# Scaling x before it is transposed, with prepared expert weights and a re-planned instruction order, in an attention, Sinkhorn-routing and expert kernel

## The chip, the cores and the metric

The kernel runs on one core of one Trainium2 chip. The metric is the device time of one execution, in microseconds (us); lower is better. Before the change, the first four runs gave a median of 1021.72 us (1018.52 to 1023.25).

## The reference

The program does attention with a window, then a mixture of eight experts in which every token passes through every expert, weighted by a Sinkhorn-normalised routing table.

```python
# q_l, k_l, v_l: 8 batches x 8 heads x 512 local tokens x 64;  q_g, k_g, v_g: 32 global tokens
# local queries see the global keys and a window of +-32; global queries see everything
x = attention(...)                      # 4352 tokens x 512
logits = x @ w_gate                     # 8 experts
P = np.exp(logits - logits.max())
for _ in range(8):                      # Sinkhorn: rows, then columns
    P /= P.sum(1, keepdims=True) + 1e-09
    P /= P.sum(0, keepdims=True) + 1e-09
    P *= N / E
out = np.zeros((N, D))
for e in range(E):
    h = np.maximum(x @ w1[e], 0.0)      # 512 -> 1024
    out += P[:, e:e + 1] * (h @ w2[e])  # 1024 -> 512
```

(The code is cut to what matters.) Since P is positive, `P * (relu(x @ w1) @ w2)` equals `relu((P * x) @ w1) @ w2`. The kernel uses this: it scales x, not the result.

## The kernel before

The program has four stages. **Attention** (32 pairs of heads) takes about the first 190 us. It is not limited by TensorE: each pair is a chain that passes between TensorE, ScalarE and VectorE. So the matmuls of **expert 0** are spread in its gaps; in the source and below they are called filler. Expert 0 is computed without its routing weight at that point (the weight is applied later), so it needs no routing. The **routing** follows: a serial chain of small VectorE steps and eight pairs of tiny TensorE column sums, `pcs`, again with expert 0 as filler. Then come 119 **units** (17 groups of 256 tokens, first with experts 1 to 3, then with 4 to 7), each made of 14 half-size products in the manner of Strassen. The **switch** between the two passes lies at about 540 to 640 us.

The order of instructions on every engine is fixed when the program is built, by a small list planner in the kernel. It works from planned durations and latencies, and each engine then runs its list in order:

```python
    def run_schedule(window=10**6):
        while pending:
            best = None
            for o in pending[:window]:
                ...
                t = ready(o)                       # when dependencies and buffers are planned free
                if t is None:
                    continue
                end, eng = min((max(t, free.get(e, 0.0)) + us, e) for e, us in o.eng.items())
                c = (max(t, free.get(eng, 0.0)), o.key)   # earliest start first, then priority
                if best is None or c < best[0]:
                    best = (c, o, eng, end)
            ...
            free[eng] = end
            o.end = end + o.lat
```

Attention operations have keys below 1000; expert 0's matmuls have keys from 1000 up, so they come second on a tie. The load of expert 0's weights (two transfers, 4 MB read) is planned as 12 us of the DMA queue:

```python
    def load_w0():
        nc.gpsimd.tensor_copy(out=tick, in_=stage[1, "q"][:, 0, 0:1])
        nc.gpsimd.dma_start(out=w1_0, in_=moe_w1[0].rearrange("(dko dki) f -> dki dko f", dki=P))
        nc.gpsimd.dma_start(out=w2_0, in_=moe_w2[0].rearrange("(fko fki) d -> fki fko d", fki=P))

    w0 = op("DMA", 12.0, load_w0, 3.6, [ops_load[1, "q", 0], ops_load[1, "k", 0]], lat=DMAL)
```

In the expert stage x is held transposed in DRAM (`xTd`), and VectorE multiplies it by the routing weights, which are broadcast over partitions (`pb`), twice per unit. The weights of experts 4 to 7 are loaded in halves of 512 KB by DMAs that convert from fp32 to fp16:

```python
    def prep(k, n_):
        ...
        if n_ < 2:
            pb = pbs[n, g][:, e - PASSES[n][0]].rearrange("p a c -> p (a c)")
            ks = slice(DK * n_, DK * (n_ + 1))
            nc.vector.tensor_tensor(out=x[:, ks], in0=xgs[n, g][:, ks],
                                    in1=pb.unsqueeze(1).broadcast_to([P, DK, 256]), op=ALU.mult)
        ...   # n_ 2 to 4: three sums and differences of x for the Strassen products

    def add_late_w(e, pool, tag, xpool, xtag, u0, before1, before2):
        at = TU * (u0 - 3)
        mk("LW1", e, "DMA2", 6.0, lambda: load_w1(e, pool(), tag), at, before1, lat=DMAL)
        mk("LW2", e, "DMA2", 6.0, lambda: load_w2(e, pool(), tag), at, [("LW1", e), *before2], lat=DMAL)
        ...   # then eight VectorE combinations of the weights
```

The softmax here doesn't subtract the row's maximum and nothing guards it: scores larger than these inputs give would overflow.

Of the kernel before, what the change touches and what calls it, by code (L numbers as in the profile page):

```python
# [17 lines left out]
def kernel(  # L18
# [51 lines left out]
    identity32 = persist.tile([P, P], FP32)  # L70
    xT = fill.tile([P, DP, NTOK], FP16, bufs=1)
# [6 lines left out]
    xTd = dram.tile([GN, P, DP, 256], FP16)  # L78
    ws = {}

    def load_w1(e, pool, tag=""):
        w1r = pool.tile([P, 4, DK, F // 2], FP16, tag="w1r" + tag, bufs=1, name="w1r")
        src = moe_w1[e].rearrange("(dko dki) f -> dki dko f", dki=P)
        for f in (0, 1):
            nc.gpsimd.dma_start(out=w1r[:, 2 * f : 2 * f + 2].rearrange("p a k x -> p (a k) x"),
                                in_=src[:, :, F // 2 * f : F // 2 * (f + 1)])
        ws[e] = [w1r, None, None]

    def load_w2(e, pool, tag=""):
        wb = ws[e][1] = pool.tile([P, 7, FK, Dhalf], FP16, tag="wb" + tag, bufs=1, name="wb")  # L90
        src = moe_w2[e].rearrange("(fko fki) d -> fki fko d", fki=P)
        for c in (0, 1):
            nc.gpsimd.dma_start(out=wb[:, 2 * c : 2 * c + 2].rearrange("p a k x -> p (a k) x"),
                                in_=src[:, :, Dhalf * c : Dhalf * (c + 1)])
# [28 lines left out]
    def op(eng, us, fn, key, deps=(), alloc=None, uses=(), lat=0.15):  # L123
        o = Op()
        o.eng = eng if isinstance(eng, dict) else {eng: us}
        o.fn, o.key, o.deps, o.alloc, o.lat, o.end = fn, key, [x for x in deps if x is not None], alloc, lat, None
        users[o] = [o]
        for u in uses:
            if u is not None:
                users[u].append(o)  # L130
                o.deps.append(u)
        pending.append(o)
        return o
# [3 lines left out]
    def ready(o):  # L137
        t = 0.0
        for x in o.deps:
            if x.end is None:  # L140
                return None
            t = max(t, x.end)
        if o.alloc:
            tag, n = o.alloc
            h = heads.setdefault(tag, [])
            if len(h) >= n:
                for x in users[h[-n]]:
                    if x.end is None:
                        return None
                    t = max(t, x.end)  # L150
        return t

    def run_schedule(window=10**6):
# [3 lines that stand above are left out]
# [6 lines left out]
                c = (max(t, free.get(eng, 0.0)), o.key)  # L163
                if best is None or c < best[0]:
                    best = (c, o, eng, end)
            (start, _), o, eng, end = best
# [7 lines left out]
    PEL, DMAL = 0.28, 2.2  # L174

# [20 lines left out]
    qkT, ugk, u_, xns, ogs, pts, pss, pgs, pos_, pqs, hTs, phs, pys = ({} for _ in range(13))  # L196
# [100 lines left out]
    def normalise(p):  # L297
# [3 lines left out]
        t = xns[p] = wk.tile([P, NM, 2, Dh], FP16, tag="xn", bufs=3, name="xn")  # L301
# [4 lines left out]
    xo = gbank[:, 0:256].bitcast(FP16)  # L306
    ptg = gbank[:, 384 : 384 + 2 * Sg].rearrange("p (a s) -> p a s", s=Sg)
# [15 lines left out]
    def normalise_g(b, hh):  # L323
        rg = wk.tile([P, 1], FP32, tag="rg", name="rg")
        nc.vector.reciprocal(out=rg, in_=pog[:, Dh:VC])
        t = ogs[b, hh] = wk.tile([P, Dh], FP16, tag="og", name="og")
        nc.vector.tensor_scalar(out=t, in0=pog[:, 0:Dh], scalar1=rg[:, 0:1], scalar2=None, op0=ALU.mult)

    def back(p):
        for m in range(NM):  # L330
            nc.tensor.transpose(xo[:, P * m : P * (m + 1)], xns[p][:, m, :, :], identity)
# [7 lines left out]
    def gate(t0, t1):  # L339
        for to in range(t0, t1):  # L340
            for dk in range(DP):
                nc.tensor.matmul(pl[:, (to - t0) * E : (to - t0 + 1) * E], xT[:, dk, P * to : P * (to + 1)],
                                 w_gate_sb[:, dk, :], start=(dk == 0), stop=(dk == DP - 1))

    def exp_gate(t0, t1):
        nc.scalar.activation(out=K_nat[:, t0:t1, :].rearrange("p t e -> p (t e)"),
                             in_=pl[:, 0 : (t1 - t0) * E], func=AF.Exp)
# [37 lines left out]
    GT = 4  # L385
    groups = [(t, min(GT, TO - t)) for t in range(0, TO, GT)]

    def h_unit(g, fm, half):
# [6 lines left out]
        for dk in range(2 * half, 2 * half + 2):  # L395
            nc.tensor.matmul(phs[g, fm][:, 0:TG], w1_0[:, dk, P * fm : P * (fm + 1)], xT[:, dk, P * g0 : P * g0 + TG],  # L396
# [19 lines left out]
    def evac_y(eng, g, c):  # L416
        t = yss[g, c] = (late["ys"] if "ys" in late else fill).tile([P, D], FP32, tag="ys", bufs=5 if "ys" in late else 2,
# [3 lines left out]
    def store_y(g, c):  # L421
        nc.gpsimd.dma_start(out=y0d[groups[g][0] + c], in_=yss[g, c])
# [3 lines left out]
    make_identity(nc, identity32)  # L426
# [22 lines left out]
    T, EQ, EK, SC, X, M, GK, XG, A, N, AG, NG, BK, EB, FL, EF, GA, GE, GO, XS = ({} for _ in range(20))  # L449
    LDORD = [(0, nm, n) for n in range(4) for nm in ("q", "k", "v") if nm != "v" or n % 2 == 1]  # L450

    def add_load(b, nm, n, of, key):
# [3 lines left out]
        ops_load[b, nm, n] = op("DMA", dma_us[nm] / of, lambda: load(b, nm, h0, h1), key, deps, lat=DMAL)  # L456
# [55 lines left out]
    def add_attend(p):  # L512
# [3 lines left out]
        A[p] = op("PE", 0.9, lambda: attend(p), k + 0.2, [M[p, 0], M[p, 1], ops_cast[b, "v", hp // 2], gv[b // 2]],  # L516
                  uses=[X[p, 0, 0], X[p, 0, 1], XG[b, hh]], alloc=("po", 1), lat=PEL)
        N[p] = op("DVE", 0.85, lambda: normalise(p), k + 0.2, uses=[A[p]], alloc=("xn", 3))
        BK[p] = op("PE", 0.24, lambda: back(p), k + 0.3, uses=[N[p]], alloc=("xo", 1), lat=PEL)
        EB[p] = op(either(0.49, 0.61), 0, lambda eng: copy_on(eng, xT[:, hp, S_tok * b + Sg : S_tok * (b + 1)], xo), k + 0.3,  # L520
                   uses=[BK[p]])
        if hp % 2 == 1:
            AG[b, hh] = op("PE", 0.36, lambda: attend_g(b, hh), k + 0.25, [A[p], XS[b // 2]],
                           uses=[X[p, 0, 0], X[p - 1, 0, 0]], alloc=("pog", 1), lat=PEL)
            NG[b, hh] = op("DVE", 0.4, lambda: normalise_g(b, hh), k + 0.25, uses=[AG[b, hh]], alloc=("og", 2))
            FL[b, hh] = op("PE", 0.15, lambda: flip(ptg, ogs[b, hh]), k + 0.35, uses=[NG[b, hh]], alloc=("ptg", 1), lat=PEL)
            EF[b, hh] = op("ACT", 0.15, lambda: nc.scalar.copy(
                out=xT[:, 2 * hh : 2 * hh + 2, S_tok * b : S_tok * b + Sg], in_=ptg), k + 0.35, uses=[FL[b, hh]])

    S_tok = Sg + Sl  # L530
# [7 lines left out]
    tick = const.tile([P, 1], FP32)  # L538

    def load_w0():  # L540
        nc.gpsimd.tensor_copy(out=tick, in_=stage[1, "q"][:, 0, 0:1])
        nc.gpsimd.dma_start(out=w1_0, in_=moe_w1[0].rearrange("(dko dki) f -> dki dko f", dki=P))
        nc.gpsimd.dma_start(out=w2_0, in_=moe_w2[0].rearrange("(fko fki) d -> fki fko d", fki=P))

    w0 = op("DMA", 12.0, load_w0, 3.6, [ops_load[1, "q", 0], ops_load[1, "k", 0]], lat=DMAL)
    add_load(1, "v", 0, 1, 3.7)

    ready_b, sched_gate = {}, 0
    for b in range(B):
# [17 lines left out]
        t0, t1 = sched_gate, (S_tok * (b + 1)) // P  # L567
        sched_gate = t1
        ready_b[b] = [EB[p] for p in range(HP * b, HP * (b + 1))] + [EF[b, 0], EF[b, 1]]
        GA[b] = op("PE", 0.55, lambda t0=t0, t1=t1: gate(t0, t1), HP * (b + 1) + 0.6, ready_b[b], alloc=("pl", 1), lat=PEL)  # L570
        GE[b] = op("ACT", 0.2, lambda t0=t0, t1=t1: exp_gate(t0, t1), HP * (b + 1) + 0.6, uses=[GA[b]])
# [11 lines left out]
    for n, (kind, g, i) in enumerate(seq):  # L583
        key = 1000.0 + n
        if kind == "h":
            us = 0.435 * groups[g][1] / GT
            if i == 0:
                htag = op("NONE", 0.0, lambda: None, -5, [w0], alloc=("hT", 2))
            u0 = op("PE", us, lambda g=g, i=i: h_unit(g, i, 0), key, [w0, *ready_b[min(g, B - 1)], before],
                    alloc=("mm", 2), uses=[htag])  # L590
            before = op("PE", us, lambda g=g, i=i: h_unit(g, i, 1), key, [u0], lat=PEL)
            r = op(either(0.5, 0.61), 0, lambda eng, g=g, i=i: relu_h(eng, g, i), -2, [before], uses=[u0])
            hops[g, i] = (u0, r, htag)
        else:
            prev = None
            for q in range(4):
                prev = op("PE", 0.435, lambda g=g, i=i, q=q: y_unit(g, i, q), key,
                          [before, *([hops[g, f][1] for f in range(FT)] if q == 0 else [prev])],
# [4 lines left out]
            ev = op(either(0.5, 0.61), 0, lambda eng, g=g, i=i: evac_y(eng, g, i), -2, [prev], uses=[first], alloc=("ys", 2))  # L603
# [3 lines left out]
    stored = []  # L607
    for g in range(GN):
        bs = range(256 * g // S_tok, (256 * g + 255) // S_tok + 1)
        stored.append(op("DMA", 0.7, lambda g=g: nc.sync.dma_start(out=xTd[g], in_=xT[:, :, 256 * g : 256 * (g + 1)]),  # L610
                         500.0 + g, [x for b in bs for x in ready_b[b]], lat=DMAL))
    all_att = [x for b in range(B) for x in ready_b[b]] + list(GE.values())

    def open_late():
# [3 lines left out]
        late["cp"] = late_pool("cp", bufs=2, side="right")  # L618
        late["ps_h"] = late_pool("ps_h", bufs=1, side="right", space=PSUM)
        late["sink"] = tc.alloc_tile_pool(name="sink", bufs=1, side="right", reuse_waits="tile")  # L620
        late["ps_c"] = tc.alloc_tile_pool(name="ps_c", bufs=1, space=PSUM, reuse_waits="tile")
        late["ys"] = tc.alloc_tile_pool(name="late_ys", bufs=1, reuse_waits="tile")
# [40 lines left out]
    R = TO * E  # L663
    ptd = dram.tile([TO, E, P], FP32)
    pn = P_nat.rearrange("p t e -> p (t e)")

    def turn(j):
        n = min(P, R - P * j)
        if j == 0:
            sk["pT"] = late["ps_c"].tile([P, 3, P], FP32, tag="cs", name="pT")  # L670
            sk["pT_sb"] = late["sink"].tile([P, 3, P], FP32, tag="pT", bufs=1, name="pT_sb")
        nc.tensor.transpose(sk["pT"][0:n, j, :], pn[:, P * j : P * j + n], identity32)

    def turn_out(j):
        n = min(P, R - P * j)
        nc.scalar.copy(out=sk["pT_sb"][0:n, j, :], in_=sk["pT"][0:n, j, :])
# [316 lines left out]
```

## Time and profile before

| | before |
|---|---|
| median of 4 runs | 1021.72 us |
| span of the profiled run | 1020.1 us |
| TensorE busy | 981.1 us (96%) |
| VectorE busy | 884.8 us (87%) |
| ScalarE busy | 672.1 us (66%) |
| moved by DMA | 119.18 MB |

These are the first line, the busy line and one line of the costliest groups from the page of the kernel before. A group's line reads: line, engine, operation, output and inputs, shape, count, then busy us in all and mean ns of one, then the engine's idle time before them and what ended it.

```profile
span 1020.1 us, 30644 instructions
...
PE 981.1 (96%) x12921; PEld 830.7 (81%) x12921; DVE 884.8 (87%) x2058; ACT 672.1 (66%) x1306; POOL 51.6 (5%) x89
...
L708 DVE TENSOR_TENSOR xp<-xg,pb 128x512 f16<-128x512 f16 x238 | 163.2, 687 | 15.4 <-PE Y L725 15.4
```

TensorE (PE) is busy nearly all the time, but its busy share hides differences between the stages. So the next view matters more: the windows view of the kernel before. Each row is a stretch of time, its length, the busy us of each engine with its number of instructions, the granted TensorE clock, the DMA share and GB/s.

```profile
core 0: us, PE busy (x) PEld busy (x) DVE busy (x) ACT busy (x) POOL busy (x), PEclk, DMA share, GB/s
...
30.00:70.00 40.00, 37.21 (x535) 21.55 (x533) 26.76 (x64) 29.16 (x64) 0.74 (x2) 0.87 0.89 247
70.00:190.00 120.00, 118.14 (x1850) 68.65 (x1849) 83.90 (x195) 91.60 (x206) 17.73 (x26) 1.00 0.76 194
190.00:300.00 110.00, 100.91 (x820) 64.24 (x819) 70.00 (x154) 57.50 (x109) 19.64 (x31) 0.97 0.70 156
300.00:540.00 240.00, 239.48 (x3219) 224.65 (x3217) 238.09 (x565) 168.22 (x320) 0.00 (x0) 1.00 0.29 92
540.00:640.00 100.00, 92.45 (x1203) 84.75 (x1200) 94.56 (x218) 60.63 (x116) 6.50 (x8) 0.98 0.55 122
640.00:1000.00 360.00, 360.00 (x4899) 341.62 (x4897) 342.65 (x803) 242.19 (x450) 0.00 (x0) 1.00 0.23 71
```

The reader should see three losses that look removable: VectorE at 238.09 of 240 us in the first pass, 92.45 of 100 us for TensorE at the switch, and 100.91 of 110 us around the routing. The next view shows what TensorE waited for at the switch (waits of TensorE, 540 to 640 us; us in total, times, longest):

```profile
PE X L725 <- ACT u3s L736: 3.0, 1, 3.0
PE X L725 <- DVE xp L708: 1.7, 2, 1.4
PE X L725 <- ACT u2s L736: 1.6, 3, 0.5
PE Z L725 <- DVE h L100: 0.9, 2, 0.5
```

A busy share does not tell a matmul at half clock from one at full clock. So I worked out a second number from the records. Each matmul is given the time that it needs at full clock: 0.417 ns for each of its columns plus 2 ns, an estimate fitted to the commonest spacing of starts in these traces (0.056 us for 128 columns, 0.109 for 256, 0.216 for 512); matmuls that use only part of the array's rows or columns are counted at their share. The **lost time** up to a moment is that moment minus the full-clock time of all the matmuls started by then. It adds up waits and half-clock time. It is an estimate, the same for all kernels, and between two profiles of one kernel it differs by up to 3 us.

| lost in, us | 0-190 (attention) | 190-300 (routing, first units) | 300-540 (pass 1) | 540-640 (switch) | 640-1000 (pass 2) |
|---|---|---|---|---|---|
| before | 67.6 | 16.0 | 5.0 | 12.4 | 2.3 |

### The profile page before, as it was taken

How to read it: one execution, taken by the hardware profiler on the slowest of the kernel's cores; microseconds unless marked ns; L12 is line 12 of the kernel's file. 1: busy time of each engine (PE TensorE's matmuls, PEld its weight loads, DVE VectorE, ACT ScalarE, POOL GpSimd, SP SyncE). 2: the span in 40 equal slices, each digit the busy share in tenths (PEclk: the TensorE clock that was granted, in tenths of full speed). 3: DMA queues.
4: the chain of work that ended last, by engine and by line, in shares of the span. 5: the costliest groups of instructions: out<-in, count | busy, mean ns of one | idle time of the engine just before them, and what ended most of it. 6: DMA issues, size and time to landing. Idle time of an engine off the chain costs nothing. (4 is left out here: it accounts for less than half of the span.)

```text
span 1020.1 us, 30644 instructions
## 1 busy us (share of the span) xinstructions
PE 981.1 (96%) x12921; PEld 830.7 (81%) x12921; DVE 884.8 (87%) x2058; ACT 672.1 (66%) x1306; POOL 51.6 (5%) x89
## 2 busy tenths in 40 slices
PE   5999999989999999999999889999999999999997
PEld 3555655434799999999999878999999999999997
DVE  5677776581599999999999899999999999999996
ACT  4678877434667766777776556666666666666664
POOL 2000030211300000000000100000000000000000
PEclk9799999989999999999999999999999999999999
DMA  9979696732962332332322791222222222222211
GB/s 266 259 219 296 203 209 135 132 119 96 226 143 80 99 94 85 94 94 93 104 76 91 141 195 59 90 73 74 74 74 74 75 74 74 74 75 73 75 43 43
DMA packets 127530, 119.18 MB, mean 117 GB/s; under 512 B 17424, under 2 KB 102944, under 8 KB 127392
## 3 DMA queue, kind: packets, MB, share of 16 engines
q1 hardware_dynamic: 99040, 91.13, 29.2%
q0 software_dynamic: 26768, 25.70, 13.4%
q8 instruction: 101, 1.65, 0.7%
q10 hardware_dynamic: 1584, 0.39, 0.2%
q14 instruction: 37, 0.30, 0.1%
HBM read 102.65 MB, written 31.33 MB: 131 GB/s over the span
## 5 line engine op out<-in xcount | busy, mean ns | idle before, releaser
L763 PE MATMUL acc<-wb,s 128*128 128x256 f16 x1904 | 275.4, 273 | 0.4 <-DVE s L100 0.3
L739 ACT ACTIVATE h<-h 128x512 f16<-128x512 f16 x357 | 224.3, 630 | 71.9 <-DVE h L100 70.1
L725 PEld LDWEIGHTS <-w1r 128*128 128x128 f16 x3808 | 245.3, 98 | 21.3 <-issue 12.4
L763 PE MATMUL acc<-wb,h 128*128 128x256 f16 x1428 | 209.9, 273 | 0.1
L725 PEld LDWEIGHTS <-w1x 128*128 128x128 f16 x2856 | 182.8, 98 | 5.3
L763 PEld LDWEIGHTS <-s 128*128 128x128 f16 x1904 | 172.5, 98 | 15.9 <-DVE s L100 0.6
L708 DVE TENSOR_TENSOR xp<-xg,pb 128x512 f16<-128x512 f16 x238 | 163.2, 687 | 15.4 <-PE Y L725 15.4
L725 PE MATMUL X<-tt,w1r 128*128 128x128 f16 x1904 | 145.5, 219 | 6.3 <-ACT u3s L736 4.6
L763 PEld LDWEIGHTS <-h 128*128 128x128 f16 x1428 | 130.2, 98 | 12.7 <-issue 1.0
L736 ACT COPY u3s<-X 128x512 f32<-128x512 f32 x119 | 69.3, 582 | 73.9 <-PE X L725 73.4
L100 DVE TENSOR_TENSOR h<-p1s,Z 128x512 f16<-128x512 f32 x119 | 81.2, 682 | 30.1 <-ACT p1s L736 28.1
L736 ACT COPY p1s<-X 128x512 f32<-128x512 f32 x119 | 69.1, 581 | 29.2 <-PE X L725 29.2
L100 DVE TENSOR_TENSOR h<-u3s,Y 128x512 f16<-128x512 f32 x119 | 81.3, 683 | 2.4 <-ACT u3s L736 2.1
L736 ACT COPY u2s<-X 128x512 f32<-128x512 f32 x119 | 68.5, 576 | 22.5 <-PE X L725 22.3
L100 DVE TENSOR_TENSOR h<-u2s,Y 128x512 f16<-128x512 f32 x119 | 81.1, 682 | 1.6 <-PE Y L725 1.6
L739 ACT ACTIVATE h<-X 128x512 f16<-128x512 f32 x119 | 70.1, 589 | 17.0 <-PE X L725 14.0
L252 ACT ACTIVATE u<-sc 128x480 f16<-128x480 f32 (+1 forms) x128 | 61.0, 523 | 22.5 <-PE sc L247 21.8
L396 PE MATMUL ph<-xT,w 128*128 128x512 f16 (+1 forms) x288 | 73.8, 373 | 1.8 <-ACT ys L200 1.1
L725 PE MATMUL X<-xp,w1r 128*128 128x128 f16 x952 | 72.6, 219 | 1.9 <-DVE xp L708 1.7
L725 PE MATMUL Z<-xp,w1r 128*128 128x128 f16 x952 | 72.6, 219 | 1.2 <-DVE h L100 1.0
L725 PE MATMUL Y<-tt,w1x 128*128 128x128 f16 x952 | 73.0, 220 | 0.0
L725 PE MATMUL X<-tt,w1x 128*128 128x128 f16 x952 | 72.6, 219 | 0.0
(121 smaller groups left out, 1299.0 us busy)
## 6 DMA issues: line engine op xcount, KB each, us to landing
pb<-ptd SPq DMA_DIRECT2D x119, 128.0 KB, 3.9
y0d<-ys POOLq DMA_DIRECT2D x34, 256.0 KB, 3.5
xg<-xTd SPq DMA_DIRECT2D x34, 256.0 KB, 3.6
o<-y0d SPq DMA_DIRECT2D x34, 256.0 KB, 2.8
ya<-o SPq DMA_DIRECT2D x34, 256.0 KB, 2.1
o<-ya SPq DMA_DIRECT2D x34, 256.0 KB, 3.1
out_dram<-o SPq DMA_DIRECT2D x34, 256.0 KB, 2.0
qs<-in_q_l_dram SPq DMA_DIRECT2D x7, 1024.0 KB, 7.8
```

Source lines behind the costliest of these rows:

```text
L100: nc.vector.tensor_tensor(out=o, in0=a, in1=b_, op=ALU.add)
L252: nc.scalar.activation(out=u_[p][i][:, mp, :], in_=pss[p, mp][i][:, 0:w], func=AF.Exp, scale=scale)
L396: nc.tensor.matmul(phs[g, fm][:, 0:TG], w1_0[:, dk, P * fm : P * (fm + 1)], xT[:, dk, P * g0 : P * g0 + TG], start=(dk == 0), stop=(dk == ...
L708: nc.vector.tensor_tensor(out=x[:, ks], in0=xgs[n, g][:, ks], in1=pb.unsqueeze(1).broadcast_to([P, DK, 256]), op=ALU.mult)
L725: nc.tensor.matmul(dst[:, j, :], l[:, d, P * j : P * (j + 1)], r[:, d, :], start=(first and j == 0 and d == 0), stop=(j == FK - 1 and d == ...
L736: nc.scalar.copy(out=d[k], in_=X[k])
L739: nc.scalar.activation(out=hq(k, f, t), in_=hq(k, f, t) if src is None else src, func=AF.Relu)
L763: nc.tensor.matmul(acc(i), l[:, j, :], wb[:, r, j, :], start=(e == es[0] and j == 0 and i in (1, 5)), stop=(e == es[-1] and j == FK - 1), ...
```

## The change

The intent is to take work off VectorE and to have the weights ready at the switch:

- x is stored to DRAM in natural layout, from attention's output. For each unit it is scaled there, one half on ScalarE and one half on VectorE, stored to a scratch tensor, and read back through a DMA transpose.
- The weights of experts 4 and 5 arrive in 128 KB pieces spread over pass 1. Those of 6 and 7 are converted to fp16 in DRAM in pass 1, and loaded at the switch by plain DMAs. The weights of experts 1 to 3 are converted by GpSimd.
- The planner is changed: the two w0 loads are planned on GpSimd with a long latency and take no DMA time; input loads are planned with a longer latency; dependencies between two TensorE operations lose their latency; and expert 0's matmuls carry a penalty (`PEN`), which holds them back during attention.

The core of the diff (848 lines; the rest is wiring, pool moves and the split of some groups of x between TensorE and DMA transposes):

```diff
-            t = max(t, x.end)
+            t = max(t, x.end - (x.lat if x.pe and o.pe else 0.0))
...
-                c = (max(t, free.get(eng, 0.0)), o.key)
+                c = (max(t, free.get(eng, 0.0)) + (PEN if o.pe and o.key >= 1000 else 0.0), o.key)
...
+    PEN = 0.2
...
-        ops_load[b, nm, n] = op("DMA", dma_us[nm] / of, lambda: load(b, nm, h0, h1), key, deps, lat=DMAL)
+        ops_load[b, nm, n] = op("DMA", dma_us[nm] / of, lambda: load(b, nm, h0, h1), key, deps, lat=2.2 if b == 0 else 5.0)
...
-    w0 = op("DMA", 12.0, load_w0, 3.6, [ops_load[1, "q", 0], ops_load[1, "k", 0]], lat=DMAL)
+    w0 = []
+    first = op("NONE", 0.0, lambda: None, -5, [ops_load[0, "v", 0]], lat=9.0)
+    for i in (0, 1):
+        w0 += 4 * [op("POOL", 0.9, lambda i=i: load_w0_gp(i), 3.6 + 0.01 * i, [first], lat=(13.0, 20.0)[i])]
...
+    def scale_x(eng, k, a):
+        ...
+        o, i, w = xss[k][:, a], xgs[n, g][:, a], P_nat[:, 2 * g + a, e : e + 1]
+        if eng == "ACT":
+            nc.scalar.activation(out=o, in_=i, func=AF.Copy, scale=w)
+        else:
+            nc.vector.tensor_scalar(out=o, in0=i, scalar1=w, scalar2=None, op0=ALU.mult)
+
+    def put_x(k):
+        nc.sync.dma_start(out=xsd[k % NX].rearrange("(a p) d -> p a d", p=P), in_=xss[k])
+
+    def turn_x(k):
+        xps[k] = late["cp"].tile([P, DP, 256], FP16, tag="xp", bufs=5, name="xp")
+        nc.sync.dma_start_transpose(out=xps[k], in_=xsd[k % NX])
...
-            nc.vector.tensor_tensor(out=x[:, ks], in0=xgs[n, g][:, ks], in1=pb.unsqueeze(1).broadcast_to([P, DK, 256]),
-                                    op=ALU.mult)
...
+    def cast_piece(e, i):            # experts 6 and 7: fp32 -> fp16 inside DRAM
+        d, src, n = (wd1, moe_w1, D // 8) if i < 8 else (wd2, moe_w2, F // 8)
+        r = slice(n * (i % 8), n * (i % 8 + 1))
+        nc.gpsimd.dma_start(out=d[e][r], in_=src[e][r])
```

## The prediction

> **What bounds the kernel now.** TensorE. The page gives it 981.1 us of 1020.1 busy (96%), VectorE 884.8 (87%), ScalarE 66%. By the matmul starts in the timeline, one work unit (256 tokens, one expert, fourteen products) takes 6.18 us from 640 to 1000 us, with a product starting every 0.44 to 0.45 us: this half is at its matmul rate, and the change keeps its 84 matmuls per unit. 119 units need 735.8 us; the expert stage takes 260 to about 1015.5 us, so 20 us are lost:
> - about 5 us in the first pass, where units from 12 to 30 take 6.34 us: the windows view shows VectorE busy 68.0 of 68.0 us (332 to 400);
> - about 11.5 us at the switch to experts 4-7 (560 to 640 us): waits of 2.99, 1.41 and several 0.5 us, on `u3s`, VectorE's `xp` multiply and `h`, while weights load (9.0 and 13.3 us per half); granted clock 0.93;
> - about 3 us at its start (waits of 1.28, 0.5, 0.34 us).
> Before it, 260 us hold attention, expert 0 and the routing. At 200 to 230 us TensorE waits 3.65 us behind a routing column sum (`pcs`), then gets clock 0.87. The first 50 us lose more (11.3 us idle in the first 25, clock 0.80 in the next 26), but mostly to input loads: DMA share 1.0.
>
> **What the change does.** Scaling by routing weights moves from transposed x (two VectorE multiplies per unit, 687 ns each, 163.2 us in all) to natural layout, on ScalarE or VectorE (planned 0.58 or 0.26 us per half); the result goes to DRAM and returns through a DMA transpose. Weights 4-7 are loaded in small throttled pieces beforehand, 6 and 7 converted in DRAM so that the switch needs only plain loads. Expert weights 1-3 are converted by GpSimd. Layer 1 of the first two units runs inside expert 0's tail. TensorE loses 16 of 128 transposes of `xn` and three of P (about 2 us in all).
>
> **On the critical path.** VectorE's load per first-pass unit falls by roughly 0.7 us or more, so that pass should go at 6.18: -5 us. The switch: two to four units of time for 512 KB plain loads, so -9. Sinkhorn/expert 0 and the transition: -6. Fewer TensorE transposes: -2. New stalls (GpSimd issuing in order, transpose latency, more HBM traffic, early stage): +1 to +4. The Trainium skill ("DMA: Bandwidth & Descriptors", Latency and other measured facts) gives a DMA transpose 261 GB/s; so I estimate 1 us of DMA time, plus about 4 to 5 us latency, per 6.18 us unit. No run here shows it yet. It is issued several units ahead, so it should stay hidden.
>
> **Prediction: 1000 us, range 986 to 1016.** Chances: faster by over 2% 0.57, within 2% 0.39, slower 0.04.
>
> **Right if** units of both passes take 6.18 us; VectorE falls below 85% in the first pass, total to some 750 us; no `xp` wait over 1 us; the switch loses under 3 us; no half-clock stretch at 566 us; the largest waits left lie in the first 60 us.
>
> **Wrong if** DMA transposes take over 6 us in throughput (units would stretch evenly, TensorE waiting for `xp` from DMA); in-order GpSimd delays `o` loads, so seeds of accumulators stall each group; attention slows under earlier DMA traffic or because `xT` for expert 0 comes late, leaving routing without matmuls to hide it.

## The result, and the profile after

| | before | after |
|---|---|---|
| median | 1021.29 us (16 runs, 1018.52 to 1025.16) | 1014.93 us (11 runs, 1013.23 to 1017.50) |
| ratio | | 0.9934, 95% interval 0.9921 to 0.9948 |
| profiled span | 1020.1 us | 1012.6 us |
| VectorE busy | 884.8 us (87%) | 803.1 us (79%) |
| ScalarE busy | 672.1 us (66%) | 735.9 us (73%) |
| moved by DMA | 119.18 MB | 179.30 MB |

A ratio is the mean time of one kernel's fast runs over that of the other's fast runs of the same rounds, so it is not quite the ratio of the medians quoted beside it. The change is worth 0.7%, not the forecast 2.1%.

From the page of the changed kernel, the lines that answer to those of before:

```profile
span 1012.6 us, 31574 instructions
...
PE 976.0 (96%) x12894; PEld 830.0 (82%) x12894; DVE 803.1 (79%) x1961; ACT 735.9 (73%) x1413; POOL 202.0 (20%) x401
...
L785 ACT ACTIVATE xs<-xg,P_nat 128x512 f16<-128x512 f16 x119 | 83.4, 720 | 2.3 <-DMA xsd<-xs 1.9
```

The other half of the scaling takes 347 ns (median) on VectorE. So VectorE gives up 2 x 687 ns per unit and takes back about 355, and ScalarE takes on 720. The windows view of the changed kernel, in the same stretches:

```profile
30.00:70.00 40.00, 35.07 (x489) 20.57 (x487) 27.59 (x67) 23.74 (x56) 9.20 (x14) 0.83 0.98 271
70.00:190.00 120.00, 113.01 (x1819) 65.59 (x1817) 85.08 (x204) 86.12 (x197) 32.99 (x49) 1.00 0.67 205
190.00:300.00 110.00, 105.68 (x849) 66.61 (x846) 74.75 (x162) 63.94 (x117) 29.21 (x48) 1.00 0.79 218
300.00:540.00 240.00, 238.61 (x3233) 225.53 (x3231) 210.13 (x527) 193.37 (x364) 83.05 (x196) 1.00 0.93 191
540.00:640.00 100.00, 98.27 (x1326) 92.42 (x1324) 88.90 (x219) 77.51 (x145) 9.09 (x17) 1.00 0.70 184
640.00:1000.00 360.00, 359.87 (x4888) 341.23 (x4886) 293.68 (x733) 273.68 (x503) 31.39 (x58) 1.00 0.52 132
```

The switch improves from 92.45 to 98.27 busy, and the routing from 100.91 to 105.68. The attention stage gets worse: TensorE is busy for 35.07 in place of 37.21 us from 30 to 70, and for 113.01 in place of 118.14 us from 70 to 190. In lost time:

| lost in, us | 0-190 | 190-300 | 300-540 | 540-640 | 640-1000 |
|---|---|---|---|---|---|
| before | 67.6 | 16.0 | 5.0 | 12.4 | 2.3 |
| after | 78.7 | 7.8 | 3.9 | 3.4 | 2.7 |
| difference | **+11.1** | -8.2 | -1.1 | -9.0 | +0.4 |

The sum is -6.8 us, and 1.1 us less matmul work makes it -7.9; the spans differ by 7.5. So the question has a clear form: why does attention lose 11 us more? It is not that attention ends much later: the last matmul on the values (`po`) of the last pair starts at 185.0 us before and at 185.8 us after. But by then TensorE has done 48.7 us of expert 0 in place of 56.8. So some 8 of the 11 us are filler that did not get done in that time.

At the switch the changed kernel waits for this (waits of TensorE, 540 to 640 us):

```profile
PE X L816 <- ACT u2s L827: 1.3, 1, 1.3
PE acc L854 <- DVE o L128: 0.3, 1, 0.3
```

In the attention stage it waits for something that the kernel before did not wait for. These are two timeline lines of the changed kernel, one of TensorE and one of VectorE (start us, us, engine, line, operation, and the idle time before it with its cause). Each is the longest wait of its engine between 36 and 60 us:

```profile
45.56 0.40 PE L258 MATMUL pt<-identity,kn 128*128 128x128 f16 x4 [2.30 <-DVE kn L231]
...
45.07 0.43 DVE L231 CAST kn<-ks 128x512 f16<-128x512 f32 x1 [2.51 <-DMA ks<-in_k_l_dram]
```

VectorE stood at the head of its list with a cast of batch 2's keys, whose load had not landed. It could not go on to the next thing, and TensorE, whose next matmul was the transpose of these keys, stood behind it. By the clock records, the changed kernel runs at half clock from 47.3 to 61.0 us (13.65 us), just after this wait.

DMA transposes were the feared cost. The lines of the DMA issues on the changed kernel's page (KB each where known, median us from issue to landing) show why they did not bind: 4.0 us landing against five buffers of 6.18 us each. The plain half loads at the switch land in 6.0 us (before: 9.0 and 13.3 us).

```profile
xp<-xsd SPq DMA_TRANSPOSE x119, 4.0
w1r<-wd SPq DMA_DIRECT2D x4, 512.0 KB, 6.0
```

### The profile page after: what moved, and what is told of

The parts are those of the page before. It is cut to its first block, busy times and chain, and to the rows that moved or that the text cites. A ratio compares the mean times of both kernels' runs of the same rounds, so it can differ in the third digit from the quotient of the medians.

```text
span 1012.6 us, 31574 instructions
## 1 busy us (share of the span) xinstructions
PE 976.0 (96%) x12894; PEld 830.0 (82%) x12894; DVE 803.1 (79%) x1961; ACT 735.9 (73%) x1413; POOL 202.0 (20%) x401
## 2 busy tenths in 40 slices
DMA packets 252611, 179.30 MB, mean 177 GB/s; under 512 B 156080, under 2 KB 232624, under 8 KB 251952
## 4 chain that ended last, share of the span: by engine, by line
PE 74%; DVE 10%; issue 5%; DMA 4%; ACT 3%; SPq 2%; POOL 1%; ACTq 0%; DVEq 0%; POOLq 0%
PE acc L854 31%; PE X L816 18%; PE Y L816 9%; PE Z L816 5%; PE py L479 4%; PE ph L464 3%; DMA xg<-xd 2%; SPq L426 1%; DVE h L128 1%; DVE qkT L231 1%; SPq L242 1%; DVE xn L335 1%; DVE o L128 1%; DMA w1r<-wd 1%; DMA gs<-in_k_g_dram 1%
## 5 line engine op out<-in xcount | busy, mean ns | idle before, releaser
L854 PE MATMUL acc<-wb,s 128*128 128x256 f16 x1904 | 279.1, 273 | 0.0
L816 PEld LDWEIGHTS <-w1r 128*128 128x128 f16 x3808 | 250.8, 98 | 15.0 <-issue 4.5
L854 PE MATMUL acc<-wb,h 128*128 128x256 f16 x1428 | 213.4, 273 | 0.3 <-DVE o L128 0.3
L816 PEld LDWEIGHTS <-w1x 128*128 128x128 f16 x2856 | 186.5, 98 | 8.6 <-issue 1.1
L854 PEld LDWEIGHTS <-s 128*128 128x128 f16 x1904 | 168.7, 98 | 12.4
L854 PEld LDWEIGHTS <-h 128*128 128x128 f16 x1428 | 126.7, 98 | 9.5 <-issue 0.4
L827 ACT COPY p1s<-X 128x512 f32<-128x512 f32 x119 | 69.1, 581 | 23.5 <-PE X L816 20.5
L785 ACT ACTIVATE xs<-xg,P_nat 128x512 f16<-128x512 f16 x119 | 83.4, 720 | 2.3 <-DMA xsd<-xs 1.9
L1015 POOL DMA_DIRECT2D out_dram<-o x32 | 17.4, 544 | 310.6 <-DVE o L128 307.3
L128 DVE TENSOR_TENSOR s<-h 128x512 f16<-128x512 f16 x119 | 50.1, 421 | 34.1 <-ACT h L830 27.1
L816 PE MATMUL Y<-xp,w1x 128*128 128x128 f16 x952 | 72.6, 219 | 0.2 <-DVE h L128 0.2
```

The lines of the kernel that those rows point to most:

```text
L128: nc.vector.tensor_tensor(out=o, in0=a, in1=b_, op=ALU.add)
L785: nc.scalar.activation(out=o, in_=i, func=AF.Copy, scale=w)
L816: nc.tensor.matmul(dst[:, j, :], l[:, d, P * j : P * (j + 1)], r[:, d, :], start=(first and j == 0 and d == 0), stop=(j == FK - 1 and d == ...
L827: nc.scalar.copy(out=d[k], in_=X[k])
L854: nc.tensor.matmul(acc(i), l[:, j, :], wb[:, r, j, :], start=(e == es[0] and j == 0 and i in (1, 5)), stop=(e == es[-1] and j == FK - 1), ...
L1015: (nc.sync if c == (1, GN - 1) else nc.gpsimd).dma_start(out=(ya, outr)[c[0]][2 * c[1] + a], in_=obs[c][:, a, :])
```

## The experiments

Fourteen runs were made, two of them repeats as controls; all are correct. Four questions are asked in turn: is it the order, is it the traffic of the new stores, what is the rest, and what made the gains? The labels are short names. Where an expectation speaks of theories by letter, S and O are the fixed order of instructions, F the planner's penalty on filler, I the time at which a weight load is issued, and C the traffic of the new stores of x.

### 1. The order of the attention stage

**w0dma.** In the plan, the load of expert 0's weights takes DMA time again, as it did before.

```diff
-        w0 += 4 * [op("POOL", 0.9, lambda i=i: load_w0_gp(i), 3.6 + 0.01 * i, [first], lat=(13.0, 20.0)[i])]
+        w0 += 4 * [op("DMA", 6.0, lambda i=i: load_w0_gp(i), 3.6 + 0.01 * i, [ops_load[1, "q", 0], ops_load[1, "k", 0]], lat=DMAL)]
```

> The changed kernel with one thing undone in the scheduler's plan: the two loads of expert 0's weights again occupy the planned DMA for 12 us after the loads of batch 1, instead of costing 0.9 us of GpSimd with a fixed latency. Instructions and traffic are the same, only the order on each engine moves: 55.6 us of expert-0 matmuls stand before the last attention pair instead of 48.7 (before: 56.8). Theory S (static order: the plan thinks the loads of batch 2 land early, so TensorE and VectorE queue up behind them): the loss by 70 us falls by 4 us or more and the time by 4 to 7 us, ratio to before about 0.987 to 0.990. Theory F (the filler penalty of 0.2 us keeps expert 0 out of the gaps): under 2 us gained, ratio 0.991 to 0.994. Theory C (the early stores of x compete with the input loads for DMA): no gain, ratio 0.993.

Measured: 1009.46 us, ratio 0.9864 (0.9845 to 0.9884). About half of the missing gain comes back with one line of planning. This is a little more than theory S allowed, and of the loss by 70 us only 1.3 us came back in this profile, not the 4 us expected (4 us in the repeat below). But the edit does two things: it changes the order, and it also makes the two transfers of the weights go out at 24.4 and 36.1 us, where the changed kernel issues them at 19.5 and 20.3.

**after_ctl** (the changed kernel again, on another chip) and **w0dma_again** (the same edit) are controls.

> The changed kernel unaltered, as the control on this chip. Ratio 0.992 to 0.995; if chips differ in the ratio, it is this one that the others of this group are compared with.

> The kernel of w0dma again, beside the control. If its gain is real it stays 0.4 to 0.8% below the control on the same chip (4 to 8 us); if it was the chip, the two are within 0.2%.

Measured: 0.9934 (0.9911 to 0.9957), exactly as at first, and 0.9867 (0.9845 to 0.9889). Both hold on a second chip.

**w0plan** separates the two effects: the plan, and so TensorE's order, is w0dma's, but both transfers go out early, as in the changed kernel (at 18.0 and 19.0 us).

```diff
-        w0 += 4 * [op("POOL", 0.9, lambda i=i: load_w0_gp(i), 3.6 + 0.01 * i, [first], lat=(13.0, 20.0)[i])]
+        op("POOL", 0.9, lambda i=i: load_w0_gp(i), 3.6 + 0.01 * i, [first], lat=(13.0, 20.0)[i])
+        w0 += 4 * [op("DMA", 6.0, lambda: None, 3.6 + 0.01 * i, [ops_load[1, "q", 0], ops_load[1, "k", 0]], lat=DMAL)]
```

> Same TensorE order as w0dma, but both loads of expert 0's first weights are issued as early as in the changed kernel (second one near 20 us instead of 36). Theory O (the static order made TensorE and VectorE stand waiting for batch 2's loads): ratio to before 0.985 to 0.990, as w0dma, lost TensorE time at 100 us near 50 us. Theory I (only the later issue of the second weight load helped, by leaving DMA to batch 2's inputs): 0.992 to 0.995, lost at 100 us near 53 us.

**w0issue** is the opposite: the changed kernel's order, with only the second transfer held back behind a store of x (it goes out at 34.1 us).

```diff
+        if (b, hh) == (0, 1):
+            nc.gpsimd.dma_start(out=w2_0, in_=moe_w2[0].rearrange("(fko fki) d -> fki fko d", fki=P))
...
-        else:
-            nc.gpsimd.dma_start(out=w2_0, in_=moe_w2[0].rearrange("(fko fki) d -> fki fko d", fki=P))
```

> TensorE order as in the changed kernel, only the second load of expert 0's first weights is issued later, behind a store. Theory O: no gain, 0.992 to 0.995. Theory I: 0.986 to 0.990, with the first waits on batch 2's casts (2.3 us for TensorE near 45 us) gone.

Measured: w0plan 1009.34 us, ratio 0.9872 (0.9852 to 0.9891); w0issue 1014.38 us, ratio 0.9918 (0.9897 to 0.9938). The order gives the gain; the time of issue gives at most a sliver that the interval does not separate from the changed kernel's 0.9934 (w0issue fell just below the band that theory O gave, by 0.0002). In w0issue the 2.3 us wait for the keys is gone, but a wait of 1.8 us on another input cast takes its place: another load was late. In w0plan the lost time at 100 us is 48.4 us, against 48.0 before and 53.7 after.

The windows view of w0plan, two rows, shows the first of them with the clock back at 0.96 (the changed kernel: 0.83):

```profile
30.00:70.00 40.00, 34.33 (x570) 20.14 (x570) 28.50 (x68) 28.39 (x66) 8.50 (x13) 0.96 0.85 234
70.00:190.00 120.00, 113.85 (x1748) 64.75 (x1747) 84.89 (x202) 84.27 (x190) 32.30 (x47) 1.00 0.73 218
```

TensorE's busy time from 30 to 70 us is lower than the changed kernel's 35.07, yet it starts 570 matmuls in place of 489. Much of the changed kernel's busy time there is the same work at half clock. This is why lost time, not busy time, is compared.

### 2. The traffic of the new stores

**before_stores** adds to the kernel before a store of x from every pair of heads (32 of 128 KB), without using it.

```diff
+        op("POOL", 0.7, lambda: nc.gpsimd.dma_start(
+            out=xdx[S_tok * b + Sg : S_tok * (b + 1), 2 * Dh * hp : 2 * Dh * (hp + 1)].rearrange("(m p) d -> p m d", p=P),
+            in_=xns[p].rearrange("p m i d -> p m (i d)")), k + 0.5, [N[p]], lat=DMAL)
```

> The kernel before, plus 32 stores of the normalised attention output to DRAM (128 KB each, from GpSimd's queue, read by nobody), as the change stores x; the order on TensorE is unchanged. Results stay right. Theory C: attention slows by 4 to 10 us, ratio 1.004 to 1.010, with input loads landing later by some us between 25 and 70 us. Theories S and F: under 2 us, ratio 0.999 to 1.002.

Measured: 1029.19 us, ratio 1.0048 (1.0026 to 1.0070). By the number this is a hit for theory C, but it is not clean: the GpSimd list runs in order, and the weight load moved from 18.8 to 24.3 us, behind the first store. **before_stores2** makes the stores depend on the weight load (`[N[p], w0]` in place of `[N[p]]`), so that the load goes first.

> The first try at adding the stores of x to the kernel before let a store stand ahead of expert 0's weight load on GpSimd's queue (24.3 instead of 18.8 us). Here the weight load comes first and only the 32 stores remain as a difference. Theory C (traffic and the queue of the stores slow attention): still 3 us or more slower, ratio 1.003 to 1.006. If the delayed weight load was the cause: ratio 0.999 to 1.001.

Measured: 1033.35 us, ratio 1.0101 (1.0082 to 1.0120), worse still. VectorE waited 7.3 us for a buffer of x, because its store stood behind the 4 MB load on the same queue, and TensorE 6.2 us in turn. The changed kernel has buffers of twice the size and no such wait. So neither run isolates the traffic; together they show only that one GpSimd queue for big loads and small stores can cost 5 to 10 us.

**stores_twice** asks it from the other side: the changed kernel with each of the 256 KB stores done twice.

```diff
-        nc.gpsimd.dma_start(out=xd[r0 : r0 + Sl, ...
+        for xs_ in (xd, xdx):
+            nc.gpsimd.dma_start(out=xs_[r0 : r0 + Sl, ...
```

> The changed kernel with every 256 KB store of x to DRAM done twice, 4 MB more written in the attention stage. Theory C (the traffic and issue of these stores cost the attention stage its time): 3 us or more on top, ratio 0.996 or more. Theory O (order, not traffic): within 1.5 us of the changed kernel's 0.9934.

Measured: 1021.19 us, ratio 0.9988 (0.9968 to 1.0008), which is 5.5 us over the changed kernel (0.0054 of 1022). By the number on record that is a hit for the traffic theory and a miss for mine. The trace narrows it. Up to 160 us the lost time is 71.6 against 70.0 us in the changed kernel. Then one wait appears, with half the clock for 6.8 us from 168 us on (waits of TensorE, 155 to 192 us):

```profile
PE gbank L414 <- DMA xG<-xd: 3.7, 1, 3.7
```

The DMA transpose of x for the last groups' gate came late, because it waits for all stores of its batches. The changed kernel has no such wait in that stretch. So doubled stores do cost 5.5 us, mostly by pushing one transpose past its use; that single stores cost anything of the kind is not shown by this run. The next section comes back to it: sched4 has the same wait with single stores.

### 3. What is left: the filler held back

**pen0** sets the planner's penalty on expert 0 to zero in the changed kernel (`PEN = 0.0`).

> The changed kernel with the penalty on expert-0 matmuls in the plan set from 0.2 to 0: 72.8 us of expert-0 matmuls stand before the last attention pair instead of 48.7. Theory F: attention keeps its pace, about 8 us more filler fits in its gaps, the time falls by 5 to 8 us, ratio about 0.986 to 0.989. Theory S: the stall behind batch 2's loads stays, attention only ends later by what is filled in; within 2 us of the changed kernel, ratio 0.991 to 0.996; it may even lose, as less filler is left for the routing.

Measured: 1034.84 us, ratio 1.0118 (1.0100 to 1.0136): much slower, and outside the bands of both theories. But attention is as good as it was before: 67.8 us lost at 190 us. The loss comes later. Before the last attention pair TensorE has done 72.8 us of expert 0, where the changed kernel has done 48.7, and then too little is left to cover the routing, the first scaling and the first weights. TensorE waits, from 255 to 350 us:

```profile
PE acc L854 <- DVE s L128: 8.2, 1, 8.2
PE X L816 <- ACT u3s L827: 5.6, 2, 5.0
PE Z L816 <- POOL w1r L1031: 4.8, 2, 3.2
```

**sched4** takes back all four planner changes at once: w0dma's edit, `PEN = 0.0`, no latency discount between TensorE operations, and the shorter planned latency of loads.

```diff
-            t = max(t, x.end - (x.lat if x.pe and o.pe else 0.0))
+            t = max(t, x.end)
...
-    PEN = 0.2
+    PEN = 0.0
...
-        ops_load[b, nm, n] = op("DMA", ..., lat=2.2 if b == 0 else 5.0)
+        ops_load[b, nm, n] = op("DMA", ..., lat=DMAL)
```

> The changed kernel with all four changes to the plan's model of the attention stage undone (expert-0 weight load on the DMA, no penalty, full latency between two TensorE operations, input loads landing after 2.2 us): 56.8 us of expert-0 matmuls before the last pair, exactly as in the kernel before. All data movement of the change stays. If the lost 10 us are a matter of the static order (S, F or both), attention runs as before and the time falls by 6 to 9 us, ratio 0.985 to 0.988. If they come from the traffic and the new copies (C), the loss stays: ratio 0.992 to 0.994.

Measured: 1014.39 us, ratio 0.9918 (0.9892 to 0.9944). It recovers 5.0 us of attention (73.7 us lost at 190) and gives the same back from 190 to 300 us (12.8 in place of 7.8). The waits named there are seven on the column sums `pcs`, 3.4 us in all. The ratio lies between the two bands and nearer to that of theory C: with the filler of the kernel before, and no penalty, attention still loses 6.1 us more than it did. The trace names part of it (waits of TensorE, 155 to 192 us):

```profile
PE gbank L412 <- DMA xG<-xd: 2.1, 1, 2.1
```

This is the wait on the new DMA transpose of x that stores_twice had. The half clock follows, for 3.4 us from 166.7 us on. Together these are 3.8 of the 6.1 us, by the measure. So in this order the new path of x does cost attention time.

**w0pen01** and **w0pen005** are w0dma with a smaller penalty (0.1 and 0.05 us in place of 0.2), to find what the remaining 5 us are.

> w0dma with the planner's penalty on expert 0's matmuls halved from 0.2 to 0.1 us, so 63.7 us of expert 0 stand ahead of the last attention pair instead of 55.6. If the penalty, which holds expert 0 back, is what is left of the slower attention stage: lost TensorE time at 190 us 67 to 71 us (w0dma 76 and 73, before 67.6), and either a ratio of 0.982 to 0.986, or the same as w0dma with the gain given back between 190 and 300 us because too little of expert 0 is left. If waits of the new stores or transposes are what is left: 73 to 76 us at 190 us.

> The same with 0.05 us, 64.6 us of expert 0 ahead of the last pair. Penalty: lost at 190 us 66 to 71 us, then more given back at 190 to 300 us than with 0.1 (10 us or more in that stretch against 7 in w0dma). Stores and transposes: 73 to 76 us at 190 us.

Measured: 1019.34 us, ratio 0.9976 (0.9951 to 1.0000), and 1019.76 us, ratio 0.9981 (0.9964 to 0.9998). At 190 us they have lost 67.5 and 68.3 us, as the penalty theory said, and as little as the kernel before. All new stores and transposes of x are present in both. So a smaller penalty is enough to bring the rest of the attention loss back. That does not clear the traffic: these two kernels have 7 to 8 us more of expert 0 in attention than the kernel before, and filler can cover a wait. At equal filler there is only sched4, which does lose time to the new path, but it also plans with other latencies, so the two are not separated. The total is worse, as the second branch of the expectation said, only by more than "the same": it is given back between 190 and 350 us. For w0pen01 the waits of TensorE from 255 to 330 us begin with

```profile
PE acc L854 <- DVE s L128: 4.1, 1, 4.1
```

and it has half the clock for 6.8 us at 265 us. The whole account, in lost time:

| us lost in | expert 0 before the last pair | 0-190 | 190-300 | 300-540 | 540-640 | ratio |
|---|---|---|---|---|---|---|
| before | 56.8 | 67.6 | 16.0 | 5.0 | 12.4 | 1 |
| after | 48.7 | 78.7 | 7.8 | 3.9 | 3.4 | 0.9934 |
| after_ctl | 48.7 | 78.8 | 6.4 | 3.0 | 3.7 | 0.9934 |
| w0issue | 48.7 | 78.0 | 7.9 | 5.3 | 3.7 | 0.9918 |
| w0dma | 55.6 | 75.9 | 7.4 | 3.4 | 3.9 | 0.9864 |
| w0dma_again | 55.6 | 72.8 | 7.0 | 5.1 | 3.3 | 0.9867 |
| w0plan | 55.6 | 72.8 | 6.1 | 4.0 | 3.8 | 0.9872 |
| sched4 | 56.8 | 73.7 | 12.8 | 3.3 | 3.5 | 0.9918 |
| w0pen01 | 63.7 | 67.5 | 17.1 | 8.3 | 3.6 | 0.9976 |
| w0pen005 | 64.6 | 68.3 | 19.4 | 8.0 | 3.6 | 0.9981 |
| pen0 | 72.8 | 67.8 | 30.3 | 15.8 | 2.6 | 1.0118 |

Expert 0 is a stock of about 117 us of matmuls. Each microsecond of it that is spent in attention is not there after it, and it is only partly free there: from w0plan to w0pen01 attention takes up 8.1 us more of it, and its last `po` matmul starts 4.7 us later (186.9 and 191.6 us). Among the kernels with the change, the next two stages lose 9 to 13 us together while up to 55.6 us are spent before the last pair; with 56.8 us it is 16, with 63.7 us 25, with 72.8 us 46. The best of these kernels spend 55.6 us. w0dma and w0plan beat both the kernel before (by 1.3%) and the changed one (by 0.6 to 0.7%), w0dma on two chips.

### 4. What made the gains

**dvemul** puts two VectorE multiplications of the old size back into each unit, with a result that is not used, and tells the planner so. Everything else, the prepared weights too, stays as in the changed kernel.

```diff
         if n_ == 2:
+            for ks in (slice(0, DK), slice(DK, DP)):
+                dm = late["cp"].tile([P, DK, 256], FP16, tag="dm", bufs=1, name="dm")
+                nc.vector.tensor_tensor(out=dm, in0=x[:, ks], op=ALU.mult,
+                                        in1=K_nat.rearrange("p t e -> p (t e)")[:, 0:256].unsqueeze(1).broadcast_to([P, DK, 256]))
...
-            mk(("V", n_), k, "DVE", (0.335, 0.2, 0.2)[n_ - 2], ...
+            mk(("V", n_), k, "DVE", (1.535, 0.2, 0.2)[n_ - 2], ...
```

> The changed kernel with the two VectorE multiplies per unit (128x512, about 690 ns each) put back as dead work, planned with their time. If relief of VectorE is what the first pass and the switch gained, the units of the first pass go back from 6.18 to 6.3 us or more in part and the switch (560 to 640 us) loses several us more than in the changed kernel: 4 to 10 us slower than the control. If the gain at the switch comes from the weights prepared beforehand, the switch still loses under 5 us and the whole costs 1 to 3 us.

Measured: 1036.75 us, ratio 1.0138 (1.0119 to 1.0157), 21 us over the changed kernel, where 4 to 10 were expected. Two rows of its windows view:

```profile
300.00:540.00 240.00, 238.72 (x3160) 219.02 (x3159) 237.17 (x555) 207.49 (x388) 87.91 (x194) 1.00 0.85 186
540.00:640.00 100.00, 93.53 (x1209) 84.80 (x1207) 96.77 (x224) 75.95 (x144) 9.64 (x18) 0.98 0.65 176
```

VectorE is full again in pass 1 (237.17 of 240), and the lost time there is 9.3 us (3.9 in the changed kernel), at the switch 11.8 (3.4), in pass 2 7.7 (2.7). The run overstates, since a unit's VectorE work is now the old multiplications plus the new scaling: VectorE is busy for 913 us in all (885 in the kernel before), and passes 1 and 2 lose more than the 5.0 and 2.3 us that they lost there. How much of the 11.8 us is due to this surplus was not tested. But prepared weights alone do not make the switch short when VectorE is this full.

**swcast** is the other half: VectorE stays relieved, but experts 6 and 7 are loaded at the switch by converting DMAs straight from the fp32 input, without any preparation.

```diff
-            nc.sync.dma_start(out=ws[e][0][:, 2 * i : 2 * i + 2].rearrange("p a k x -> p (a k) x"),
-                              in_=wd1[e].rearrange("(k p) f -> p k f", p=P)[:, :, F // 2 * i : F // 2 * (i + 1)])
+            nc.gpsimd.dma_start(out=ws[e][0][:, 2 * i : 2 * i + 2].rearrange("p a k x -> p (a k) x"),
+                              in_=moe_w1[e].rearrange("(k p) f -> p k f", p=P)[:, :, F // 2 * i : F // 2 * (i + 1)])
...
-            while npc < 64 and 4 + npc * 0.66 <= u:
+            while npc < 32 and 4 + npc * 0.66 <= u:
```

> The changed kernel, but the last two experts' weights are again loaded at the switch straight from fp32 by a casting GpSimd DMA, with no pieces converted beforehand. If weights prepared beforehand made the gain at the switch, the stretch 540 to 640 us loses 5 us or more again and the ratio is 0.998 or more. If VectorE's relief made it, the stretch loses about 3.5 to 5 us and the ratio stays within 2 us of 0.9934 (0.9915 to 0.9953).

Measured: 1022.83 us, ratio 1.0000 (0.9983 to 1.0017). The switch loses 14.3 us. One wait of TensorE there, and the wait of VectorE (586 to 603 us, timeline) that stands behind it:

```profile
PE acc L854 <- DVE o L128: 5.0, 1, 5.0
...
594.11 0.69 DVE L128 TENSOR_TENSOR w1x<-w1r 128x1024 f16<-128x1024 f16 x1 [4.99 <-DMA w1r<-in_moe_w_dram]
```

VectorE stands for 5 us at the head of its list with a combination of weights that have not landed, and the sums that TensorE needs stand behind it. So the gain at the switch needs both parts: with either one taken away, the switch loses about as much as before (11.8 and 14.3 us, before 12.4, after 3.4). Neither run is the old arrangement: dvemul loads VectorE more, and in swcast the converting loads share GpSimd's queue with the loads and stores of `o`, which the kernel before issued from SyncE.

## Why the prediction was wrong

The forecast was 1000 us, and 1014.93 was measured. The time is inside the range of 986 to 1016 because the range is wide, but the change of -0.7% is a third of the forecast -2.1%. Point by point:

| the prediction's term | forecast, us | measured, us | verdict |
|---|---|---|---|
| pass 1 at full rate | -5 | -1.1 | right in sign, a fifth of the size |
| the switch | -9 | -9.0 | right in size; it takes VectorE's relief as well as the plain loads that the term names |
| routing and transition | -6 | -8.2 | right in sign, but it is paid for (below) |
| fewer TensorE transposes | -2 | -1.1 | right in sign, half the size |
| "New stalls (GpSimd issuing in order, transpose latency, more HBM traffic, early stage): +1 to +4" | +1 to +4 | +11.1 in attention | **wrong: the step that failed** |

**The failing step is the term for new stalls in the early stage.** It was mis-sized by 7 us or more, and the causes that it lists are not the main ones that were found in the changed kernel. The +11.1 us split into two parts, by w0plan of about the same size.

- *About 3 to 6 us: the order.* The changed planner gives the 4 MB load of expert 0's weights no DMA time, so it believes that batch 2's keys and queries land early, and puts their casts and transposes ahead of expert 0's matmuls. On the chip they land late, and in-order VectorE and TensorE stand waiting (2.51 and 2.30 us at 45 us), with half the clock for 13.65 us just after. w0plan changes this order alone and goes from 78.7 to 72.8 us (the two profiles of w0dma: 75.9 and 72.8); w0issue changes the time of issue alone and goes to 78.0.
- *About 5 us or more: the penalty.* It holds expert 0 back (48.7 us done before the last pair, where the kernel before had 56.8). w0pen01 lowers it, and attention is back at 67.5 us with all the new traffic in place. Whether the new path of x has a share in these 5 us, hidden in w0pen01 by more filler, stays open (sched4). This part is not waste: it buys the better routing stage. The prediction booked the routing's -6 as a free gain and did not see that attention would pay for it from the same stock.

I had named "attention slows" among the things that could make me wrong, but with the DMA traffic or a late `xT` as its cause and a bare routing stage as its result. The runs show a wrong model of a load in the planner, and a routing stage that got better at attention's expense.

**The second miss is pass 1.** I gave it 5 us because VectorE was full from 332 to 400 us (68.00 of 68.0). The units at 6.34 us, which I read as going "from 12 to 30", in fact end near 427 us, and all of pass 1 lost only 5.0 us. Of that, 3.9 remain, since new waits came: four of TensorE on ScalarE's copy `u2s`, 1.4 us in all (300 to 540 us), where ScalarE's busy time rose from 168 to 193 us, as it now does half the scaling at 720 ns each (I read 0.58 from the plan). That the scaling causes these waits is read from the trace and was not tested alone. dvemul fits the view that VectorE's relief matters here: pass 1 loses 9.3 us when each unit has more VectorE work than in the kernel before.

**What was right.** The switch; that it agrees to a tenth of a microsecond is luck, since the measure is not that sharp, and the experiments show that it takes both relief and preparation. The DMA transposes of the units stayed hidden. My estimate from the Trainium skill ("DMA: Bandwidth & Descriptors", Latency and other measured facts: 261 GB/s for a DMA transpose with a non-contiguous middle dimension, more for a contiguous one) was 1 us of DMA time; the trace has 4.0 us (median of 119) from issue to landing in all, and TensorE never waits over 0.5 us for a transposed `xp`. There is no half clock at 566 us any more, and the longest waits left are indeed early (the 2.3 us shown is the longest after the first 25 us). Three marks were missed: VectorE is at 88% in pass 1 (210.13 of 240), not below 85%; its total fell to 803 us, not 750, and the half of the scaling that stays on it alone is 41.6 us; the switch loses 3.4 us, where I named 3.

**The routing.** What the kernel before lost there can be read from its VectorE timeline (204 to 210 us). A combination of expert weights stands in the middle of the Sinkhorn chain and waits for its load:

```profile
205.67 0.69 DVE L97 TENSOR_TENSOR wb<-wb 128x1024 f16<-128x1024 f16 x1 [2.01 <-DMA wb<-in_moe_w_dram]
206.28 0.63 DVE L651 TENSOR_REDUCE cp<-t 128x8 f32<-128x272 f32 x1
```

TensorE's longest wait on `pcs` there is 3.6 us, and half the clock holds from 204.1 us for 6.8 us; the changed kernel's longest is 1.5 us, at full clock. No experiment moved this alone, so it stays a reading of the trace.

**Half clock.** The Trainium skill ("TensorE: Matmul & The Clock Gate", What's actually happening) says that this gate sets the clock to either full or half, that it is decided in free-running windows of 3413 ns, and that at least one idle window brings the half clock. All half-clock stretches here, after the start-up and before the end, are multiples of 3.413 us (one to five of them, 3.4 to 17.1 us), which agrees. Their place and length differ from run to run of one kernel (after: one of 13.65 us; after_ctl: three of 3.41 between 37 and 61 us; w0dma 20.5 us in all and w0dma_again 6.8), which may explain part of the spread in the first stage. The kernel before had 10.24 us of it there, as much as after_ctl, so the half clock alone is not why attention lost more.

**Left open.** How much the new stores and transposes of x cost attention in the changed kernel: w0pen01 loses no more at 190 us than the kernel before, within the measure's spread of up to 3 us, but with more filler; sched4 waits 2.1 us for one transpose; and no run takes the stores away. The attention stage could not be improved and the routing kept covered at once by any setting tried; a plan that spends the stock with measured latencies in both stages was not built.

## What to carry to other kernels

When instruction order is fixed by a planner, a change of the plan's model (a load that takes no DMA time, a latency, a penalty) is a change of the kernel, and has to be costed like one. Work that fills gaps is a stock: before booking a gain in one stage, ask which other stage the filler was taken from. An engine with an in-order list makes everything behind a late load late, so look first at the head of the list when the engine that stands still is not the one that is short of time.

## What the Trainium skill lacked or had wrong

- "TensorE: Matmul & The Clock Gate" (What's actually happening) ties the half clock to at least one idle window of about 3.4 us. Here it came without one: in the kernel before it began at 36.8 us although no wait of TensorE from 22 us on was longer than 1.1 us, and in w0plan at 37.0 us, after seven microseconds with TensorE busy for 5.05 us and no wait over 1.2 us. A later section of that page (A second HAM failure mode: psum-queue depth-cycling) does describe a clock that changes with frequent short idles; it gives no length for them.
- "SBUF — State Buffer" (Who interferes with whom) says that a VectorE instruction with two SBUF inputs contends with a GpSimd instruction that reads SBUF. The trace of the changed kernel agrees, and gives the size that the page has not for this pair: the routing's 128x272 fp32 multiplication takes 0.44 us alone, and 0.94 us here, when it starts 0.39 us after a GpSimd conversion of weights, which lasts 1.04 us (timeline, GpSimd and VectorE):

```profile
203.95 1.04 POOL L1031 CAST w1r<-stg 128x1024 f16<-128x1024 f32 x1 [0.80 <-DMA stg<-in_moe_w_dram]
204.34 0.94 DVE L748 TENSOR_TENSOR t<-K_nat,rv 128x272 f32<-128x272 f32 x1
...
206.67 0.44 DVE L748 TENSOR_TENSOR t<-K_nat,cv 128x272 f32<-128x272 f32 x1
```

- "DMA: Bandwidth & Descriptors" (Latency and other measured facts) gives a rate for the DMA transpose but no time from issue to landing. Here 256 KB from DRAM took 4.0 us (median of 119), about 3 us more than the estimate of 1 us from the rate. Plain transfers of 256 KB took medians of 2.4 to 5.1 us in the same kernel.
- No page has a way to cost filler: here a stock of about 117 us of matmuls, where 55.6 us spent before the last attention pair gave 0.987, 48.7 gave 0.993 and 72.8 gave 1.012.
